# Batch 0's last 192 rows behind four gate products, and gate products over 384 tokens, then 128

## The chip, the cores and the metric

One NeuronCore of one Trainium2 chip runs the whole program. The metric is the time of one execution in microseconds. Three runs of the kernel before give a median of 340.75 us (340.57 to 342.16).

## What is computed

The reference is sliding-window attention with ALiBi slopes, and behind it a gated feed-forward block:

```python
B, H, S, D = 8, 8, 576, 64;  window = 128
scores = q @ k.T / 8 - slope[h] * |i - j|          # only 0 <= i - j < 128
attn   = softmax(scores) @ v                       # per batch and head
x      = attn as 4608 tokens x 512
out    = (gelu(x @ w_gate) * (x @ w_val)) @ w_out  # 512 -> 1536 -> 512
```

Inputs and output are float32 in HBM; the kernel works in bf16 with float32 sums.

## The kernel before

**Tiling.** The 4608 tokens are eight batches of 576. Attention runs batch by batch, the feed-forward block in nine groups of 512 tokens, so group 0 lies wholly in batch 0. The hidden width of 1536 is cut into twelve tiles of 128, called f = 0 to 11. `gate_val(g, f, lo, hi)` makes "one gate product": four matmuls with a tile of `w_gate` and four with the same tile of `w_val`, over tokens lo to hi of group g, then a gelu on ScalarE (L612) and a multiplication into `hT` on VectorE (L613). With its argument `later` the gelu and the multiplication are put in a list and issued where the list is emptied.

**Order.** The order of instructions on each engine is the order in which the code writes them; no scheduler changes it. Every engine takes its own list in order, and waits for semaphores of the others. PSUM has eight banks of 512 columns; `bank()` hands them out in turn as they come free. Loads that turn float32 into bf16 are all issued by GpSimd on one queue. At most eight of them are under way: each issue waits for the one eight places before it.

**The opening stage, batch 0.** Rows 0 to 383 of q and k come first, as float32 on SyncE's and ScalarE's queues, and are cast, transposed on TensorE and scored pair of heads by pair of heads (`c` = 0 to 3; L798 to L808). `exp` (L219) writes the probabilities. Sums over them (`sums_first`), their reciprocals as Ln and Exp on ScalarE (`inverse_first`, L559 and L560), the products with v (`values_first`) and the scaling (`scale_first`, L563) give the tokens 0 to 383 of `xT`.

Batch 0's last 192 rows are a second part. Their q and k are loaded by `load_runs(0, 1, 0, 8)` into the tile `vb[1]`, 64 rows for each of q and k, three tokens to a row. VectorE's cast copy (L814) puts them into `pairs1`, a part of the tile `wo`. `rest` (L761) transposes them and copies them into qT and kT (L158). `scores0_rest` (L348) makes scores and exps for given pairs of heads and puts masks in a list, which `flush` issues (L222). `products_rest` (L573) makes sums and products with v, `inverse_rest` (L582) takes one reciprocal on VectorE for each c (L584), `scale_rest` (L586) makes tokens 384 to 575 of `xT` (L587). So group 0 needs these for its last 128 tokens. Before, the gate products of f = 0 and 1 over 384 tokens stand between the scores of the rest, f = 2 to 8 over 384 tokens behind `products_rest`, then f = 0 to 8 over tokens 384 to 511, then f = 9 to 11 over all 512 (in the loop over g).

`decays` writes the mask's exponentials of a head, `masks_of_last_blocks` copies them to further columns of `emask`. `transpose(1, w, c, copy)` transposes batch 1's q and k on TensorE (L150) once `load_runs(1, n, 0, 8)` has brought them. `preload_act_table_set` loads ScalarE's table for exp and Ln; a gelu behind an exp, or the other way round, has a table load ahead of it.

**Behind it.** The loop over g does the remaining gate products of a group, then the steps of `todo`: scores and values of later batches between the output products (L642, L662).

Of the kernel before, what the change touches and what calls it, by code (L numbers as in the profile page):

```python
# [30 lines left out]
def kernel(  # L31
# [10 lines left out]
    nc = tc.nc  # L42
    B, H, S, D = q.shape
# [72 lines left out]
    def load_v(b, js=range(5)):  # L116
        load(vb[b % 2], v, b, js, 64)
# [12 lines left out]
    def load_runs(b, n, h0, h1):  # L130
        first, parts, r = RUNS[b][n]
        for what, src in ((0, q), (1, k)):
            nc.gpsimd.dma_start(
                out=runs(what, b, n)[:, h0:h1, :],
                in_=src[b][h0:h1, first:first + parts * r, :].rearrange(
                    "h (p r) d -> p h (r d)", r=r))
# [412 lines left out]
    def sums_first(c, u=0):  # L549
        return [(u + x, slice(c, c + 2), n0 * x, n0 * x + n0, 0) for x in (0, 1)]  # L550
# [5 lines left out]
    def inverse_first(c, x, ps):  # L556
        to = recip[0][:, c:c + 2, n0 * x:n0 * x + n0]
        src = ps[:, 0:2 * n0].rearrange("p (c x) -> p c x", c=2)
        return (lambda: nc.scalar.activation(out=to, in_=src, func=AF.Ln),  # L559
                lambda: nc.scalar.activation(out=to, in_=to, func=AF.Exp, scale=-1.0))  # L560
# [143 lines left out]
                   allow_small_or_imprecise_dtypes=True)  # L704
    nc.gpsimd.memset(ones64, 1.0)
    nc.gpsimd.tensor_copy(out=mark, in_=raw[0][0][0:1, 0:2])
    load_runs(0, 1, 0, 8)
    load_v(0, (0, 1, 2))
    load_w(0, 128)
    load_w(128, 256)  # L710
    load_v(0, (3, 4))
    load_w(256, 512)

    for h in range(H):
        nc.vector.memset(slope1[:, h:h + 1], -8.0 * 2.0 ** (-8.0 * (h + 1) / H))
# [45 lines left out]
    def rest(copies):  # L761
        pss = [bank().bitcast(BF16) for _ in range(2)]
        for c in (0, 2):
            for w, ps in enumerate(pss):
                p = 64 * w
                for n in (c, c + 1):
                    for x in range(3):
                        nc.tensor.transpose(
                            out=ps[:, 192 * n + 64 * x:192 * n + 64 * x + 64],
                            in_=pairs1[p:p + 64, x, 128 * n:128 * n + 128],  # L770
                            identity=ident[p:p + 64, p:p + 64])
# [4 lines left out]
    nc.scalar.preload_act_table_set("natural_log_exp_and_others")  # L776
    held = [bank(), bank()]
    keep_busy(held[0], 2, 128)
    keep_busy(held[0], 60)
# [27 lines left out]
    scores0((2,), biases)  # L807
    scores0((3,), biases0((3,)))  # L808
    row(0)
    sums_a = products(0, sums_first(0))  # L810
    for step in zip(*(inverse_first(0, x, sums_a[x]) for x in (0, 1))):
        for do in step:
            do()
    dve(out=pairs1.rearrange("p x (h d) -> p h x d", d=64),  # L814
        in_=vb[1].rearrange("p j x -> p (j x)")[:, 0:1536].rearrange(
            "p (h x d) -> p h x d", h=H, x=3))
    load_w(512, 768)
    load_w(768, 1024)
    load_w(1024, 1280)
    for n in (0, 1):  # L820
        load_runs(1, n, 0, 8)
    load_w(1280, DFF)
    masks, waiting = [], []

    def flush():
# [1 line left out]
            mask(*args)  # L827
        masks.clear()

    rest((dve, dve))  # L830
    sums_b = products(0, sums_first(2))
    for x in (0, 1):
        ln, minus = inverse_first(2, x, sums_b[x])
        ln()
        decays(5 + x, 6 + x)
        minus()
    decays(7, 8)
    vals = products(0, values_first(0) + values_first(2, 2))
# [12 lines left out]
    waiting = waiting[2:] + waiting[:2]  # L851
    for later in waiting:
        later()
    waiting.clear()
    for _ in range(2):
        bank()
    pss = products_rest()
    inverse_rest(0, pss)
    for f in range(2, 9):
        gate_val(0, f, 0, 384)  # L860
        if f < 5:
            inverse_rest(f - 1, pss)
        if f == 5:
            scale_rest()
    masks_of_last_blocks(0, 8)
    for f in range(9):
        gate_val(0, f, 384, 512)
    for n in range(2):
        nc.gpsimd.dma_start(
            out=wo[:, 6 * n:6 * n + 6, :],  # L870
            in_=moe_w_out[768 * n:768 * n + 768, :].rearrange("(c p) f -> p c f", p=128))
# [24 lines left out]
                ("add", b, 2), 4]  # L896


    def exp_table():
        nc.scalar.preload_act_table_set("natural_log_exp_and_others")  # L900

    RUN = {"s": scores, "s2": scores2, "add": add, "sum4": sums4, "gather": gather, "spread": spread_dma, "pv": values, "pv+": values_and_sums,
           "masks": flush, "table": exp_table, "transposes": transposes_dma, "last": out_last, "o": out_half}

    for g in range(NG):
        if 1 <= g < B - 2:
            transposes_dma(3 if g == 1 else g + 2)
        if g == 1:

            nc.gpsimd.tensor_copy(out=mark, in_=qT[1][0:1, 0, 512:514])  # L910
            load_qk(4)
            load_v(3)
        for f in range(9 if g == 0 else 0, NF):
            gate_val(g, f)
            if g == 0 and f in (9, 11):
                for c in (0, 1) if f == 9 else (2, 3):
                    for w in (0, 1):
                        transpose(1, w, c, (act, dve)[w])
# [59 lines left out]
```

## Time and profile before

| what | us |
|---|---|
| median of three runs | 340.75 |
| the profiled execution | 342.65 |
| its span, first to last instruction | 340.8 |
| TensorE matmul busy | 332.9 (98%) |
| VectorE busy | 190.8 (56%) |
| ScalarE busy | 170.1 (50%) |
| GpSimd busy | 106.3 (31%) |
| mean granted TensorE clock | 0.995 |

All times below are counted from the start of the span of that execution. Engines in the profile: PE is TensorE's matmuls, PEld its weight loads, DVE VectorE, ACT ScalarE, POOL GpSimd, SP SyncE. A matmul's end is modelled, so its busy time is not its share of the peak. In the rows the form is: output tile <- input tiles, partitions x elements; buffer numbers are left out.

### The profile page before, as it was taken

How to read it: one execution, taken by the hardware profiler on the slowest of the kernel's cores; microseconds unless marked ns; L12 is line 12 of the kernel's file. 1: busy time of each engine (PE TensorE's matmuls, PEld its weight loads, DVE VectorE, ACT ScalarE, POOL GpSimd, SP SyncE). 2: the span in 40 equal slices, each digit the busy share in tenths (PEclk: the TensorE clock that was granted, in tenths of full speed). 3: DMA queues.
4: the chain of work that ended last, by engine and by line, in shares of the span. 5: the costliest groups of instructions: out<-in, count | busy, mean ns of one | idle time of the engine just before them, and what ended most of it. 6: DMA issues, size and time to landing. Idle time of an engine off the chain costs nothing.

```text
span 340.8 us, 8164 instructions
## 1 busy us (share of the span) xinstructions
PE 332.9 (98%) x3334; PEld 170.4 (50%) x3334; DVE 190.8 (56%) x358; ACT 170.1 (50%) x319; POOL 106.3 (31%) x142
## 2 busy tenths in 40 slices
PE   8899999999998999999999999999999999999996
PEld 6667655444554455445544454445444544444443
DVE  7669566344689637943695369535974323303320
ACT  6973598537894328433753357344823133223322
POOL 5975763481094095007700680040000000000000
PEclk9899999999999999999999999999999999999999
DMA  8999999999699799949993999599106110020002
GB/s 215 164 186 190 205 165 152 141 182 182 135 147 160 146 185 191 185 102 154 182 187 78 165 180 192 75 162 110 64 2 140 63 62 0 3 93 31 0 33 92
DMA packets 149738, 43.49 MB, mean 128 GB/s; under 512 B 133540, under 2 KB 142660, under 8 KB 149700
## 3 DMA queue, kind: packets, MB, share of 16 engines
q0 software_dynamic: 107424, 18.10, 69.0%
q1 hardware_dynamic: 39104, 18.69, 22.8%
q10 hardware_dynamic: 3172, 6.19, 8.3%
q8 instruction: 26, 0.43, 0.5%
q14 instruction: 12, 0.10, 0.1%
HBM read 43.65 MB, written 9.53 MB: 156 GB/s over the span
## 4 chain that ended last, share of the span: by engine, by line
PE 88%; DMA 6%; ACT 2%; DVE 2%; issue 1%; POOL 0%; ACTq 0%; DVEq 0%
PE ps L606 53%; PE ps L642 23%; PE ps L484 4%; DMA rb<-rd 3%; PE ps L288 2%; DMA vb<-in_k_dram 2%; PE ps L662 2%; PE ps L206 1%; DMA wo<-in_q_dram 1%; ACT P L219 1%; PE ps L676 1%; DVE xT L541 1%; PE ps L422 1%; PE ps L150 1%; DVE hT L613 0%
## 5 line engine op out<-in xcount | busy, mean ns | idle before, releaser
L613 DVE TENSOR_TENSOR hT<-ps,gelu 128x512 bf16<-128x512 f32 (+3 forms) x119 | 74.0, 636 | 94.9 <-PE ps L606 89.6
L612 ACT ACTIVATE gelu<-ps 128x512 bf16<-128x512 f32 (+3 forms) x119 | 65.3, 558 | 105.2 <-PE ps L606 95.4
L606 PE MATMUL ps<-xT,wg 128*128 128x512 bf16 (+3 forms) x476 | 113.9, 360 | 0.3
L606 PE MATMUL ps<-xT,wv 128*128 128x512 bf16 (+3 forms) x476 | 113.8, 360 | 0.0
L642 PE MATMUL ps<-wo,hT 128*128 128x512 bf16 x396 | 90.3, 380 | 0.0
L606 PEld LDWEIGHTS <-wv 128*128 128x128 bf16 x476 | 45.6, 98 | 48.6
L606 PEld LDWEIGHTS <-wg 128*128 128x128 bf16 x476 | 44.8, 98 | 48.3 <-issue 0.3
L642 PEld LDWEIGHTS <-hT 128*128 128x128 bf16 x396 | 37.0, 98 | 43.7
L219 ACT ACTIVATE P<-ps 128x512 bf16<-128x512 f32 (+1 forms) x108 | 51.3, 579 | 1.9 <-PE ps L206 1.6
L222 DVE TENSOR_TENSOR P<-P,emask 128x768 bf16<-128x768 bf16 x60 | 31.3, 555 | 19.3 <-ACT P L219 17.7
L647 ACT COPY osb<-ps 128x512 f32<-128x512 f32 x28 | 16.4, 587 | 50.7 <-PE ps L642 50.6
L108 POOL DMA_DIRECT2D vb<-in_v_dram x40 | 34.0, 886 | 6.9 <-DMA ks<-in_k_dram 1.8
L108 POOL DMA_DIRECT2D qs<-in_q_dram x30 | 25.2, 857 | 5.8 <-DMA wo<-in_moe_w_out_dram 4.0
L108 POOL DMA_DIRECT2D ks<-in_k_dram x30 | 25.4, 894 | 0.5 <-DMA qs<-in_q_dram 0.5
L929 POOL COPY mark<-hT 1x2 bf16<-1x2 bf16 x4 | 0.7, 174 | 79.4 <-DVE hT L613 79.4
L541 DVE TENSOR_TENSOR xT<-ps,rb 128x512 bf16<-128x512 f32 (+3 forms) x34 | 14.6, 500 | 6.3 <-PE ps L484 4.8
L484 PE MATMUL ps<-P,vb 64*64 64x192 bf16 (+2 forms) x752 | 17.5, 225 | 0.2
L484 PEld LDWEIGHTS <-vb 64*64 64x64 bf16 x752 | 14.9, 110 | 3.1 <-issue 2.6
L373 DVE TENSOR_TENSOR T<-P 64x1024 bf16<-64x1024 bf16 x20 | 13.7, 686 | 0.6
L288 PEld LDWEIGHTS <-kT 64*64 64x64 bf16 x440 | 7.7, 107 | 4.6 <-issue 4.5
L425 DVE RECIPROCAL r<-ps 128x128 f32<-128x128 f32 (+1 forms) x10 | 9.8, 1020 | 0.0
L612 ACT ACT_TABLE_LOAD x7 | 9.0, 1283 | 1.3 <-PE ps L606 1.3
(90 smaller groups left out, 182.8 us busy)
## 6 DMA issues: line engine op xcount, KB each, us to landing
out_dram<-osb SPq DMA_DIRECT2D x35, 256.0 KB
rb<-rd ACTq DMA_DIRECT2D x10, 576.0 KB
vb<-in_v_dram POOLq DMA_DIRECT2D x32, 128.0 KB, 6.6
qs<-in_q_dram POOLq DMA_DIRECT2D x24, 128.0 KB, 5.7
ks<-in_k_dram POOLq DMA_DIRECT2D x24, 128.0 KB, 6.3
wo<-in_moe_w_out_dram POOLq DMA_DIRECT2D x2, 768.0 KB, 14.8
wg<-in_moe_w_gate_dram POOLq DMA_DIRECT2D x5, 256.0 KB, 8.4
wv<-in_moe_w_val_dram POOLq DMA_DIRECT2D x5, 256.0 KB, 9.0
```

The source lines that it names most:

```text
L108: nc.gpsimd.dma_start(out=t[at:at + n, j, :].rearrange("p (h d) -> p h d", h=H), in_=src[b][:, 128 * j:128 * j + n, :].rearrange("h p d -> ...
L219: nc.scalar.activation(out=dst, in_=src, func=AF.Exp, scale=0.125)
L222: nc.vector.tensor_tensor(out=dst, in0=dst, in1=m, op=ALU.mult)
L288: mm = nc.tensor.matmul(out=ps[64 * x:64 * x + 64, col:col + w], lhsT=keys(b, c, m)[half, :], rhs=qT[b % 2][half, c, q0:q0 + w], start=Tru ...
L373: nc.vector.tensor_tensor(out=to[half, :, x:x + 7:2], in0=P[half, :, 0:10:3], in1=P[half, :, 1:11:3], op=ALU.add)
L484: mm = nc.tensor.matmul(out=out, lhsT=lhsT, rhs=prob(b)[half, c, i, col:col + q1 - q0], start=all(t[2] != u for t in todo[:n]), stop=True, ...
L541: nc.vector.tensor_tensor(out=xT[:, c, at:at + e - a], in0=src, in1=recip[b][:, c, a:e], op=ALU.mult)
L606: nc.tensor.matmul(out=ps, lhsT=w[:, c, 128 * f:128 * (f + 1)], rhs=xT[:, c, t0 + lo:t0 + hi], start=begins, stop=(c == 3), skip_group_che ...
L612: nc.scalar.activation(out=gl[:, 0:n], in_=pg, func=AF.Gelu)
L613: nc.vector.tensor_tensor(out=hid[g][:, f, lo:hi], in0=pv, in1=gl[:, 0:n], op=ALU.mult)
L642: nc.tensor.matmul(out=acc[g], lhsT=hid[g][:, f, 128 * t:128 * (t + 1)], rhs=wo[:, f, :], start=(f == 0), stop=(f == NF - 1))
L647: (nc.vector.tensor_copy if g < B - 2 and t in by_dve.get(g, (0,)) else nc.scalar.copy)(out=osb, in_=acc[g])
```

## The change

Group 0's order is written anew:

- GpSimd loads v's first three blocks and the weights of f = 0 to 3, each as 128 columns, ahead of batch 0's last 192 rows of q and k; v's last two blocks follow.
- The weights of f = 10 and 11 are loaded ahead of batch 1's q and k.
- Both lots of sums follow each other, then all reciprocals, then the remaining decays, then values and scaling.
- Gate products of f = 0 and 1 (two halves of 192 tokens), 2 and 3 (384 tokens) stand ahead of the cast copy, `rest` and the scores of the last rows. An exp table is loaded behind f = 3's gelu, and gelu's again behind the exps.
- f = 4 stands between the scores of the last rows and `products_rest`; f = 5 to 11 over 384 tokens follow. Reciprocals come behind f = 5 to 8, the scaling behind f = 9, the mask copies behind f = 10.
- Then all twelve f over tokens 384 to 511, with batch 1's transposes behind f = 8 and f = 11; the loop over g does no gate product of group 0 any more.

```diff
-    load_runs(0, 1, 0, 8)
     load_v(0, (0, 1, 2))
-    load_w(0, 128)
-    load_w(128, 256)
+    for f in range(4):
+        load_w(128 * f, 128 * f + 128)
+    load_runs(0, 1, 0, 8)
     load_v(0, (3, 4))
-    load_w(256, 512)
...
     row(0)
-    sums_a = products(0, sums_first(0))
-    for step in zip(*(inverse_first(0, x, sums_a[x]) for x in (0, 1))):
-        for do in step:
-            do()
-    dve(out=pairs1.rearrange("p x (h d) -> p h x d", d=64),
-        in_=vb[1].rearrange("p j x -> p (j x)")[:, 0:1536].rearrange(
-            "p (h x d) -> p h x d", h=H, x=3))
     load_w(512, 768)
     load_w(768, 1024)
     load_w(1024, 1280)
+    load_w(1280, DFF)
     for n in (0, 1):
         load_runs(1, n, 0, 8)
-    load_w(1280, DFF)
...
-    rest((dve, dve))
-    sums_b = products(0, sums_first(2))
+    sums = [products(0, sums_first(c)) for c in (0, 2)]
     for x in (0, 1):
-        ln, minus = inverse_first(2, x, sums_b[x])
-        ln()
-        decays(5 + x, 6 + x)
-        minus()
-    decays(7, 8)
+        for c in (0, 2):
+            for do in inverse_first(c, x, sums[c // 2][x]):
+                do()
+    decays(5, 8)
     vals = products(0, values_first(0) + values_first(2, 2))
     for x in (0, 1):
         for c in (0, 2):
             scale_first(c, x, vals[c + x])
-    scores0_rest((0,), masks)
-    gate_val(0, 0, 0, n0, waiting)
-    scores0_rest((1,), masks)
-    gate_val(0, 0, n0, 2 * n0, waiting)
+    for x in (0, 1):
+        for f in (0, 1):
+            gate_val(0, f, n0 * x, n0 * x + n0)
+    gate_val(0, 2, 0, 384)
+    gate_val(0, 3, 0, 384, waiting)
+    dve(out=pairs1.rearrange("p x (h d) -> p h x d", d=64),
+        in_=vb[1].rearrange("p j x -> p (j x)")[:, 0:1536].rearrange(
+            "p (h x d) -> p h x d", h=H, x=3))
+    waiting.pop()()
+    exp_table()
+    rest((dve, dve))
+    scores0_rest((0, 1), masks)
     flush()
     scores0_rest((2, 3), masks)
     flush()
-    gate_val(0, 1, 0, n0, waiting)
-    gate_val(0, 1, n0, 2 * n0, waiting)
-    waiting = waiting[2:] + waiting[:2]
-    for later in waiting:
-        later()
-    waiting.clear()
-    for _ in range(2):
-        bank()
+    gate_val(0, 4, 0, 384)
     pss = products_rest()
-    inverse_rest(0, pss)
-    for f in range(2, 9):
+    for f in range(5, NF):
         gate_val(0, f, 0, 384)
-        if f < 5:
-            inverse_rest(f - 1, pss)
-        if f == 5:
+        if f < 9:
+            inverse_rest(f - 5, pss)
+        if f == 9:
             scale_rest()
-    masks_of_last_blocks(0, 8)
-    for f in range(9):
+        if f == 10:
+            masks_of_last_blocks(0, 8)
...
+    for f in range(NF):
         gate_val(0, f, 384, 512)
+        if f in (8, 11):
+            for c in (0, 1) if f == 8 else (2, 3):
+                transposes_1(c)
...
-        for f in range(9 if g == 0 else 0, NF):
+        for f in range(NF if g == 0 else 0, NF):
             gate_val(g, f)
```

`transposes_1(c)` calls `transpose(1, w, c, ...)` for w = 0 and 1, with the copy of q's on ScalarE and of k's on VectorE, as the loop over g did before.

More of the change, by code (lines that the diff above doesn't have):

```diff
@@ L706 @@
     nc.gpsimd.tensor_copy(out=mark, in_=raw[0][0][0:1, 0:2])
+    load_v(0, (0, 1, 2))
+    for f in range(4):
+        load_w(128 * f, 128 * f + 128)
     load_runs(0, 1, 0, 8)
-    load_v(0, (0, 1, 2))
-    load_w(0, 128)
-    load_w(128, 256)
     load_v(0, (3, 4))
-    load_w(256, 512)
     for h in range(H):
@@ L774, in rest, with exp_table @@
                 untangle(copies[w], 0, 1, w, c, c + 2, ps[:, 192 * c:768])
-    nc.scalar.preload_act_table_set("natural_log_exp_and_others")
+    def exp_table():
+        nc.scalar.preload_act_table_set("natural_log_exp_and_others")
+    exp_table()
     held = [bank(), bank()]
@@ L841 @@
             scale_first(c, x, vals[c + x])
-    scores0_rest((0,), masks)
-    gate_val(0, 0, 0, n0, waiting)
-    scores0_rest((1,), masks)
-    gate_val(0, 0, n0, 2 * n0, waiting)
+    for x in (0, 1):
[7 more added lines that the diff above has]
+    waiting.pop()()
+    exp_table()
+    rest((dve, dve))
+    scores0_rest((0, 1), masks)
     flush()
@@ L848, with transposes_1 @@
     flush()
-    gate_val(0, 1, 0, n0, waiting)
-    gate_val(0, 1, n0, 2 * n0, waiting)
-    waiting = waiting[2:] + waiting[:2]
-    for later in waiting:
-        later()
-    waiting.clear()
-    for _ in range(2):
-        bank()
+    gate_val(0, 4, 0, 384)
     pss = products_rest()
-    inverse_rest(0, pss)
-    for f in range(2, 9):
+    for f in range(5, NF):
         gate_val(0, f, 0, 384)
-        if f < 5:
-            inverse_rest(f - 1, pss)
-        if f == 5:
+        if f < 9:
+            inverse_rest(f - 5, pss)
+        if f == 9:
             scale_rest()
-    masks_of_last_blocks(0, 8)
-    for f in range(9):
+        if f == 10:
+            masks_of_last_blocks(0, 8)
+    def transposes_1(c):
+        for w in (0, 1):
+            transpose(1, w, c, (act, dve)[w])
+    for f in range(NF):
         gate_val(0, f, 384, 512)
+        if f in (8, 11):
+            for c in (0, 1) if f == 8 else (2, 3):
+                transposes_1(c)
     for n in range(2):
@@ L896, in steps @@
                 ("add", b, 2), 4]
-    def exp_table():
-        nc.scalar.preload_act_table_set("natural_log_exp_and_others")
     RUN = {"s": scores, "s2": scores2, "add": add, "sum4": sums4, "gather": gather, "spread": spread_dma, "pv": values, "pv+": values_and_sums,
@@ L912 @@
             load_v(3)
-        for f in range(9 if g == 0 else 0, NF):
+        for f in range(NF if g == 0 else 0, NF):
             gate_val(g, f)
[L915 to L918, printed above, removed]
             if 2 <= g < B - 1:
```

## The prediction

> **What bounds the kernel now.** I read the page's 40 slices first. Each digit is a tenth of a slice of 8.5 us.
>
> ```profile
> PE   8899999999998999999999999999999999999996
> ...
> PEclk9899999999999999999999999999999999999999
> ```
>
> TensorE is busy to nine tenths nearly everywhere, so a change can win only where it isn't. The granted clock has one dip, in the second slice (8.5 to 17 us). Next the chain of work that ended last (start, length, what), cut to the stage that the change touches:
>
> ```profile
> 5.19 6.70 DMA vb<-in_k_dram
> ...
> 19.02 1.63 ACT P L219 x4
> ...
> 22.73 15.20 PE ps L606 x136
> ```
>
> The reader is to see the DMA of batch 0's last 192 rows of k, landed at 11.9, and the exps of the last rows at 19.02. Between the two the chain runs over the cast L814 and the transposes, behind the exps over a table load, a gelu and its multiplication. Only at 22.73 does a run of gate products begin that nothing interrupts. TensorE's timeline (start, length, what, idle before) shows what that costs:
>
> ```profile
> 12.61 0.60 PE L768 MATMUL ps<-ident,wo 64*128 64x64 bf16 x24 [1.05 <-DVE wo L814]
> ...
> 21.29 0.41 PE L484 MATMUL ps<-P,ones 64*64 64x256 bf16 x6 [0.56 <-DVE P L222]
> ```
>
> 1.05 us idle for the cast and 0.56 us for the last mask. And the windows of one microsecond (length, busy time per engine, granted clock as the first number after POOL's):
>
> ```profile
> 14.00:15.00 1.00, 1.00 (x50) 1.00 (x46) 1.00 (x3) 1.00 (x3) 1.00 (x2) 0.60 1.99 170
> 15.00:16.00 1.00, 1.00 (x40) 0.97 (x30) 0.68 (x3) 1.00 (x4) 1.00 (x3) 0.50 2.15 146
> 16.00:17.00 1.00, 1.00 (x9) 0.88 (x7) 1.00 (x3) 1.00 (x4) 1.00 (x2) 0.50 1.48 158
> 17.00:18.00 1.00, 1.00 (x19) 0.62 (x17) 0.85 (x2) 0.26 (x2) 1.00 (x2) 0.69 1.41 179
> ```
>
> The clock fell to half some 3.4 us after the idle began: lost 0.40 + 0.50 + 0.50 + 0.31 = 1.7 us. So some 3.3 us can be won here (1.05 + 0.56 + 1.7), if no new wait comes.
>
> **The skill against the trace.** "TensorE: Matmul & The Clock Gate", Part 1, says that the clock is judged in free-running windows of some 3.4 us, halved after an idle one. The dip, 14.0 to 17.4 by the windows, agrees in length, but the window ahead of it was not idle: 10.6 to 14.0 held two products, a pause and 0.60 us of transposes. I go by the trace: a window about half empty can halve the clock. "ScalarE: Activation LUTs", What ACT_TABLE_LOAD costs, gives some 2.66 us for a switch, drain included. Here:
>
> ```profile
> 20.66 1.28 ACT L612 ACT_TABLE_LOAD   x1
> 21.96 1.09 ACT L612 ACTIVATE gelu<-ps 128x192 bf16<-128x192 f32 x4
> ...
> 45.67 3.23 ACT L219 ACTIVATE P<-ps 128x384 bf16<-128x384 f32 x8
> ```
>
> The load takes 1.28 us, and the gelu starts 0.02 us after it. I take 1.3 us for each of the two loads that are added (exp and gelu around the last rows' exps). The last row gives eight exps of 384 in 3.23 us.
>
> **Part by part.** Times are of the changed kernel, in the same execution's clock. Up to 10.5 nothing on TensorE, ScalarE or VectorE changes its order.
>
> *Loads.* The 192 rows' q and k (384 KB as landed) go from the head of GpSimd's queue behind v (384 KB) and the weights of four products (1,024 KB). Two DMA issues are added (4 x 0.77 us in place of 2 x 0.77).
>
> ```profile
> 21.57 0.87 POOL L133 DMA_DIRECT2D ks<-in_k_dram  x1 [0.41 <-issue]
> ```
>
> k was issued at 5.19 and landed by 11.9, with 384 KB queued up to it. The row is an issue that must wait for the DMA eight places earlier, wv of products 2 and 3: landed by 21.5, with 1,984 KB queued up to it. That is 167 KB per us, so 1,792 KB, the new place of k, land at 11.9 + 1408/167 = 20.3. Bounds: at 195 KB per us (stretch of 24 to 26 us) 19.1, at 154 (10 to 12 us) 21.0. By the same line v is there by 12, the weights of product 3 by 18.1 (needed at some 19), those of 4 and 5 stay where they were (23.9). The last weights move ahead of batch 1's runs: these come 512 KB later, some 3 us, against 35.6 before, and their transposes now start after 41: hidden.
>
> *What TensorE does meanwhile.* The second sums follow the first as soon as the last exp ends (11.90), so 0.4 us idle in place of 1.05. Then values (about 0.95 us at full clock), which end near 13.7. ScalarE has Ln and Exp four times in dependent turns (0.93 us a pair), three decays (0.26 each) and a table load: gelus start near 17.9. VectorE's four scalings (0.47 each) wait for those exps, the last ends near 16.3. Products 0 to 3 start at 14.2, take 2.7 + 2 x 1.30 us and wait some 0.5 for the scalings: they end near 20.0, or 21.0 if the clock halves again at 14. Dropping the two skipped banks removes no instruction. Four gelus of 192 tokens at 0.25, product 2's at 18.9 (0.5) and its multiplication (0.5) keep VectorE until 19.9. The added wait is thus the cast for k, at C = max(19.9, 20.3) = 20.3. Behind it on VectorE stand product 3's multiplication, the four copies and all masks; on TensorE everything from the transposes on.
>
> *From C on*, with VectorE's rows of before:
>
> ```profile
> 11.99 0.56 DVE L814 COPY wo<-vb 128x1536 bf16<-128x1536 bf16 x1 [1.72 <-DMA vb<-in_k_dram]
> 13.16 0.56 DVE L158 COPY qT<-ps 128x384 bf16<-128x384 bf16 x1 [0.61 <-PE ps L768]
> ...
> 25.07 1.34 DVE L584 RECIPROCAL T<-ps 128x192 f32<-128x192 f32 x1
> ```
>
> Cast 11.99 to first copy 13.16, so C+1.17; the copies follow each other by 0.47 and take 0.55, so the second ends at C+2.2, the last at C+3.13. Scores of the first two pairs need the second: C+2.25. From the start of 12 score matmuls to their exp was 0.47 us (17.48 to 17.95): C+2.72. Eight exps: C+5.95. Only 0.9 us of scores and product 4 (1.30) lie beside them, where before two products were spread between. Last mask 0.02 + 0.56: C+6.53, products_rest at C+6.58, for 1.1 us (21.29 to 22.4), so product 5 starts at C+7.7 and ends at E = C+9.0. Table load and gelu of product 4 (C+7.7) hide under that.
>
> *Reciprocals.* They now follow products 5 to 8. A reciprocal and a multiplication take 25.07 to 26.74, 1.675 us, more than a product's 1.30. VectorE starts the first at E+0.62 (product's end 0.20, multiplication 0.42), three pairs later the last at E+5.65, the scaling L587 at E+7.32, done E+8.26. TensorE has six products, E+7.8, and then needs those tokens: waits to E+8.30, 0.5 us. Before, the scaling ended at 31.02 and was needed at 31.83, when the products over 128 tokens began. Behind it: a multiplication, four mask copies (1.42), another multiplication, which frees a bank at E+10.5; TensorE wants it at E+10.3: 0.24 us more.
>
> *The rest.* Twelve products over 128 tokens at 0.449 = 5.4; two lots of batch 1's transposes at 1.15 = 2.3. The 24 extra matmuls (384 + 128 for 512: 162.5 + 56.1 against 216.5 ns) cost 0.05 us. Batch 1's scores start at C + 9.0 + 8.3 + 5.4 + 0.24 + 2.3 = C+25.25 = 45.55; before at 43.71: **+1.8 us**. Behind that point the order is the same and TensorE is packed, so it stays.
>
> *Clock.* From 20.9 to 24.2 TensorE has 0.6 us of transposes, 0.9 of scores and two pauses: as empty as the window that brought the dip. I take half clock up to 27.6, which falls on product 4 (idle time follows: free) and 0.7 us of products_rest: **+0.35**. Bounds: 0, and 1.7 if the half clock falls on a whole window of gate products.
>
> Sum +2.15 us. The profiled execution was 342.65 (span 340.8, 1.85 around it), the median 340.75; the difference is laid on the median: **342.9**. What a measurement can't tell from no change is 0.5%, 1.7 us: 339.05 to 342.45.
>
> **Rivals.** *A, the forecast*, 0.52, itself 342.2 to 344.0.
> *B, better covered*, 0.18: k lands by 19.1, so C is VectorE's 19.9 (-0.4), the clock holds (-0.35) and the bank is free in time (-0.24): 341.9. For it: 195 KB per us is measured from 20 us on. Against: 154 to 178 before.
> *C, late rows and half clock*, 0.20: k at 21.0 (+0.7) and a window of 3.4 us at half clock on dense products (1.7 in place of 0.35): 345.0. For it: more descriptors of small size, since products 2 and 3 now load 128 columns at a time; one dip is there already. Against: the window's phase must fit.
> *D, the other side*, 0.10: rows and VectorE are ready so early that the transposes follow product 3 at once, and the idle time and half clock of before come back with no wait in their place. It decides at C = 20.3 - 2.15 = 18.15; at C = 16 the time is 338.6. For it: the cover of four products is 5.3 us long, and the 3.3 us lost are there. Against: 1,792 KB by 16 is 343 KB per us behind k's old landing, twice what was seen, and ScalarE's table load ends at 17.9.
> That the change doesn't do what it says has no chance of its own: the order of instructions shows each move.
>
> **How the numbers follow.** Faster: 0.06 (most of D). Same: B 0.18, the low end of A 0.06, the rest of D 0.04: 0.28. Slower: 0.66. The range, 341.0 to 345.2, leaves out D and the upper half of C.
>
> **What would show it.** Right: the cast's row with idle time ended by the DMA of k near 20.3; TensorE idle about 1 us ahead of the scores and 1.6 us ahead of products_rest; a wait for VectorE at the first product over 128 tokens. Wrong: the cast before 19, or transposes with no idle time before them; products_rest waiting under 0.5 us; batch 1's scores before 44.

## The result and the profile after

The changed kernel takes 345.27 us (median of 5 runs, 344.70 to 345.82), the kernel before 341.80 beside it (5 runs, 340.57 to 343.19): 3.5 us more by the medians (ratio 1.0112, 95% interval 1.0085 to 1.0138). The forecast was 342.9 (341.0 to 345.2): the right sign, but less than two thirds of the size.

The profiled execution of the changed kernel lasted 344.83 us with a span of 343.0. From the page, the same rows as of before (each digit a tenth of a slice):

```profile
span 343.0 us, 8227 instructions
...
PE   8978799999999999999999999999999999999996
...
PEclk9999999999999999999999999999999999999999
```

The clock's dip in the second slice is gone in this execution. (Of the five, that of 345.27 us has a mean clock of 0.995 again, as the first profile of before.) TensorE now has a 7, an 8 and a 7 in the third to the fifth slice (17 to 43 us), where before there were nines. What stands there is in TensorE's timeline of the changed kernel (start, length, what, idle before and who ended it):

```profile
14.54 0.33 PE L606 MATMUL ps<-xT,wg 128*128 128x192 bf16 x2 [0.35 <-DVE xT L563]
...
21.03 0.60 PE L767 MATMUL ps<-ident,wo 64*128 64x64 bf16 x24 [0.74 <-DVE wo L840]
22.20 0.27 PE L206 MATMUL ps<-qT,kT 64*64 64x192 bf16 x2 [0.57 <-DVE qT L158]
...
26.88 0.41 PE L484 MATMUL ps<-P,ones 64*64 64x256 bf16 x6 [1.17 <-DVE P L222]
...
37.87 0.40 PE L606 MATMUL ps<-xT,wg 128*128 128x128 bf16 x4 [0.48 <-DVE xT L587]
41.40 0.38 PE L606 MATMUL ps<-xT,wv 128*128 128x128 bf16 x4 [1.35 <-DVE hT L613]
```

With three short ones (0.17, 0.20, 0.19) these waits sum to 5.22 us. The two waits of before, 1.05 for the cast and 0.56 for the last mask, have become 0.74 and 1.17, and four new ones of 0.3 us or more stand beside them. The last is the largest and was forecast at 0.24. A bank is waited for there; the multiplication that frees it stands behind the mask copies on VectorE:

```profile
38.20 0.60 DVE L744 COPY emask<-emask 128x1536 bf16<-128x1536 bf16 x1
38.72 0.82 DVE L745 COPY emask<-emask 128x1024 bf16<-128x1024 bf16 x1
39.47 1.30 DVE L748 COPY emask<-emask 64x512 bf16<-64x512 bf16 x2
40.79 2.30 DVE L613 TENSOR_TENSOR hT<-ps,gelu 128x384 bf16<-128x384 f32 x8
```

and GpSimd's timeline of the same kernel at the same time:

```profile
38.48 0.78 POOL L876 MEMSET T<- 64x512 bf16 x1
39.32 0.69 POOL L877 MEMSET P<- 128x512 bf16 x1
40.06 0.55 POOL L879 MEMSET qs<- 64x512 bf16 x1
40.56 0.66 POOL L879 MEMSET ks<- 64x512 bf16 x1
```

Four copies take 2.6 us from the start of the first to the start of the multiplication behind them, where 1.42 was reckoned, and all but the start of the first run while GpSimd fills four tiles. The 1.42 came from these rows of VectorE's timeline of the kernel before (the next multiplication starts at 33.99), where GpSimd issues nothing from 32.32 to 33.47 and fills its tiles only from 38.14 on:

```profile
32.57 0.55 DVE L745 COPY emask<-emask 128x1536 bf16<-128x1536 bf16 x1
33.04 0.42 DVE L746 COPY emask<-emask 128x1024 bf16<-128x1024 bf16 x1
33.38 0.58 DVE L749 COPY emask<-emask 64x512 bf16<-64x512 bf16 x2
```

Batch 1's scores start at 47.23, where 45.55 was forecast and 43.71 was read in the kernel before. Of these 3.52 us between the two profiled executions 2.2 are left at the end: 1.3 are given back in group 2, where the profiled execution of before was slower at two places: a wait of 0.79 us at 109.03, and scores of 1.21 us at 128.65 that take 0.87 in the changed kernel.

### The profile page after: what moved, and what is told of

Same layout as the page of the kernel before. It is cut to its first block, busy times and chain, and to the rows that moved or that the text cites. A ratio compares the mean times of both kernels' runs of the same rounds, so it can differ in the third digit from the quotient of the medians.

```text
span 343.0 us, 8227 instructions
## 1 busy us (share of the span) xinstructions
PE 332.6 (97%) x3358; PEld 171.1 (50%) x3358; DVE 191.6 (56%) x361; ACT 173.7 (51%) x324; POOL 108.4 (32%) x144
## 4 chain that ended last, share of the span: by engine, by line
PE 86%; DVE 3%; DMA 3%; POOL 3%; ACT 2%; issue 2%; DVEq 0%; ACTq 0%
PE ps L606 50%; PE ps L642 24%; PE ps L484 4%; PE ps L288 2%; DMA vb<-in_k_dram 2%; PE ps L662 2%; ACT P L219 1%; PE ps L206 1%; DMA wo<-in_q_dram 1%; PE ps L422 1%; POOL wg L140 1%; POOL wv L140 1%; POOL vb L108 1%; PE ps L676 1%; DVE T L584 1%
## 5 line engine op out<-in xcount | busy, mean ns | idle before, releaser
L484 PEld LDWEIGHTS <-vb 64*64 64x64 bf16 x752 | 14.2, 107 | 3.2 <-issue 2.6
```

Of the source, the lines that this page charges most:

```text
L484: mm = nc.tensor.matmul(out=out, lhsT=lhsT, rhs=prob(b)[half, c, i, col:col + q1 - q0], start=all(t[2] != u for t in todo[:n]), stop=True, ...
```

## The experiments

Theory at this point: the cover that was given up (the scores and two products that ran on TensorE beside the exps and filled its time) costs waits that add up one to one, and the largest is the collision of the mask copies with GpSimd's memsets. Rivals: the rows land too late; the tail (384 tokens, then 128) costs by itself; the waits are covered by others when they are taken away. The kernel before, run on the same chips, had medians of 341.0 to 341.3.

**The mask copies elsewhere** (masks_last): behind all products over 128 tokens.

```
         gate_val(0, f, 0, 384)
         ...
-        if f == 10:
-            masks_of_last_blocks(0, 8)
     ...
+    masks_of_last_blocks(0, 8)
     for n in range(2):
         nc.gpsimd.dma_start(...)
```

> The changed kernel with the mask copies of VectorE moved behind the last product over 128 tokens. Theory A (the wait of 1.35 us in front of the fifth product over 128 tokens is VectorE's mask copies, slowed by GpSimd's memsets): the wait falls under 0.2 us, batch 1's scores start 1.2 us sooner (near 46.0 in place of 47.23), the time falls by about 1.2 us. Rival B (the late rows of k make up nearly all of the loss): under 0.3 us. If the copies meet GpSimd's DMA issues at their new place they are slow there, but no product waits for them.

Measured: 343.14 us (ratio to before 1.0041, 1.0018 to 1.0065), 2.0 above the kernel before beside it, where the changed kernel was 3.5 above. The wait of 1.35 is gone, the others stay (that for the cast is 0.36 here), and gate products of group 1 start at 61.88 instead of 63.29. In VectorE's timeline of this kernel the copies, with nothing waiting for them, are

```profile
46.90 0.87 DVE L744 COPY emask<-emask 128x1536 bf16<-128x1536 bf16 x1
47.69 0.41 DVE L745 COPY emask<-emask 128x1024 bf16<-128x1024 bf16 x1
```

The first is slow here too, beside a DMA issue of GpSimd (0.87 us from 46.53), as was expected. So about 1.5 us of the loss was this wait. From the first product over 128 tokens to group 1 it is 23.91 us in place of 25.42, and the medians, each against before's beside it, differ by 1.45. The 1.51 are more than the listed 1.35 because idle time is counted from the modelled end of the matmuls ahead of it: they start at 39.67, the next would have followed by 0.22, and came at 41.40.

**The memsets elsewhere** (memsets_late): the copies stay, and GpSimd waits for the multiplication of the fifth product over 128 tokens before it fills the tiles.

```
+    nc.gpsimd.tensor_copy(out=mark, in_=hid[0][0:1, 4, 384:386])
     nc.gpsimd.memset(T[64:128, :, 0:64], 0.0)
```

> The changed kernel with GpSimd's four memsets, and the loads of batch 2 behind them, held back until the product of f = 4 over 128 tokens is written; the mask copies stay. Theory A: the four copies take 0.55, 0.42 and 2 x 0.29 us again (1.5 in all in place of 2.6), the wait of 1.35 us falls to about 0.25, as the prediction had it, the time falls by about 1.1 us. Theory C (the copies are long for another reason, for example DMA issues or TensorE's reads): copies and wait stay, time within 0.3 us.

Measured: 343.74 us (1.0071, 1.0052 to 1.0091), 2.6 above before's. VectorE's timeline:

```profile
38.62 0.55 DVE L744 COPY emask<-emask 128x1536 bf16<-128x1536 bf16 x1
39.08 0.42 DVE L745 COPY emask<-emask 128x1024 bf16<-128x1024 bf16 x1
39.42 0.58 DVE L748 COPY emask<-emask 64x512 bf16<-64x512 bf16 x2
```

and TensorE's wait behind them:

```profile
40.64 0.38 PE L606 MATMUL ps<-xT,wv 128*128 128x128 bf16 x4 [0.17 <-DVE hT L613]
```

The copies have their old length and the wait is 0.17, close to the 0.24 of the prediction. This shows the collision: the same copies at the same place, without the memsets beside them. The loads behind the memsets are held back as well, but they can't be the cause: the changed kernel issues none of them before 41.18, when the copies are done. In this run each memset takes 0.52 us. The Trainium skill, "SBUF — State Buffer", SBUF: two separate sides, says that VectorE in a two-port mode and GpSimd take one pair of ports by an exclusive lock, for a whole instruction. The rows agree: 0.82 is 0.42 plus most of a memset, and the memsets grow from 0.52 to 0.78 and 0.69, as if each had waited for the other in turn; whether these copies run in such a mode, no row here says.

**The rows' loads first** (rows_first): the loads of the last 192 rows at their old place at the head of GpSimd's queue, all else as changed.

```
+    load_runs(0, 1, 0, 8)
     load_v(0, (0, 1, 2))
     for f in range(4):
         load_w(128 * f, 128 * f + 128)
-    load_runs(0, 1, 0, 8)
```

> The changed kernel with the loads of batch 0's last 192 rows at the head of GpSimd's queue again, ahead of v and the weights. Rival B: the rows are there by 12, and the time falls by 2 us or more. Theory A: VectorE is busy with product 2 until 19.9 to 20.1, so the cast comes at most 0.5 us sooner and all else stays: 0.3 to 0.5 us. If the weights of f = 0 land later than 14.5 now, it is less.

Measured: 345.04 us (1.0116, 1.0072 to 1.0159), the changed kernel's time. VectorE's timeline:

```profile
20.35 0.60 DVE L840 COPY wo<-vb 128x1536 bf16<-128x1536 bf16 x1
21.16 0.56 DVE L613 TENSOR_TENSOR hT<-ps,gelu 128x384 bf16<-128x384 f32 x1 [0.21 <-PE ps L606]
```

The cast has no idle time before it and still starts at 20.35, since VectorE's multiplications keep it until then. Here the weights behind the rows came late instead (a wait of 0.30 us for w_val at 16.47), which delays those multiplications. In the changed kernel VectorE was free at 20.12 and waited 0.29 us for the DMA: that is all that the late landing cost in this execution.

**The kernel before, once more** (before_again), unchanged, for the scatter of its waits.

> The kernel before, unchanged, profiled again. If half clock near 14 us and the wait of 0.79 us ahead of the first sums of group 2 (near 109 us) are there in only some executions, this profile shows one of them or none and a span of 338.5 to 340.8; if they belong to the kernel, both are there and the span is 340.8 again. The forecast laid a difference worked out in a profile with both on a median of runs; executions without them would account for the median of the change being larger than the difference of the two profiles (2.2 us).

Measured: 341.25 us (1.0005, 0.9980 to 1.0030). But its profiled execution, 340.44 us, differs from the one on which the prediction was built, 342.65. TensorE's timeline of this execution:

```profile
11.46 0.60 PE L768 MATMUL ps<-ident,wo 64*128 64x64 bf16 x24
...
19.62 0.41 PE L484 MATMUL ps<-P,ones 64*64 64x256 bf16 x6 [0.72 <-DVE P L222]
...
33.05 0.38 PE L606 MATMUL ps<-xT,wv 128*128 128x128 bf16 x4 [0.26 <-DVE hT L613]
```

VectorE's:

```profile
10.33 0.83 DVE L814 COPY wo<-vb 128x1536 bf16<-128x1536 bf16 x1
```

The cast starts at 10.33 instead of 11.99 and waits for no DMA, the transposes follow without idle time, the clock stays at 1.0, and the last rows' products start at 19.62 instead of 21.29. This execution is 1.30 us ahead at group 1 and another 0.87 behind group 2, 2.17 in all. So the wait of 1.05 and the half clock, most of the 3.3 us that the change was to win, belong to some executions and not to others. In four profiles with this opening (two of before, tail_alone, tail_weights_again) TensorE's wait for the cast is 1.05, 0, 0.48 and 0, and only the first has half clock near 14 us. How often half clock comes can be read from the mean clock of every run (half clock for 3.4 us of 341 makes 0.995). Of 154 runs of the kernel before, 21 have 0.995 or less, as the first profile has, with a median of 342.67 us; the other 133 have a median of 341.04. So it came, at this place or another, in about one of seven, and these runs took 1.6 us more. All 154 reach from 339.7 to 344.8 us, with a median of 341.2; the first profile's 342.65 lies above 85% of them, the second's 340.44 is faster than nine tenths.

**The tail alone** (tail_alone): the kernel before with the products over 384 tokens up to f = 11, the mask copies after f = 10, all twelve over 128, batch 1's transposes between them. The loads keep their order.

```
-    for f in range(2, 9):
+    for f in range(2, NF):
         gate_val(0, f, 0, 384)
         ...
-    masks_of_last_blocks(0, 8)
-    for f in range(9):
+        if f == 10:
+            masks_of_last_blocks(0, 8)
+    for f in range(NF):
         gate_val(0, f, 384, 512)
+        if f in (8, 11):
+            for c in (0, 1) if f == 8 else (2, 3):
+                transposes_1(c)
```

> The kernel before with the second half of the change alone: gate products f = 2 to 11 over 384 tokens, mask copies behind f = 10, then twelve products over 128 tokens with batch 1's transposes behind f = 8 and 11. Theory A (the tail costs only because the reciprocals now come late and the mask copies meet GpSimd's memsets): here the scaling ends near 31 us and is needed at 35, the copies end near 36, ahead of the memsets at 38: no wait, time as before, within 0.4 us. Rival E (products over 128 tokens cost more than their columns say, or the transposes are late): 0.5 us or more above before.

Measured: 346.95 us (1.0162, 1.0139 to 1.0185), far off the expectation. TensorE's timeline shows one large wait:

```profile
36.83 1.46 PE L606 MATMUL ps<-xT,wg 128*128 128x384 bf16 x4 [4.42 <-DMA wg<-in_moe_w_gate_dram]
```

Products 10 and 11 are wanted some 7 us earlier than before (product 10 from 32.25 in place of 39.01), and their weights lie behind batch 1's rows in GpSimd's queue. Half clock follows, from 36.2 to 39.6 us by the windows; TensorE works in it from 36.83 on and so loses another 1.4 us. All five runs have a mean clock of 0.994 or less. This says nothing of the tail's own price, but it says what the change moves the last weights ahead of batch 1's rows for. Therefore the same with those weights moved (tail_weights_ahead, and again as tail_weights_again):

```
-    for n in (0, 1):
-        load_runs(1, n, 0, 8)
     load_w(1280, DFF)
+    for n in (0, 1):
+        load_runs(1, n, 0, 8)
```

> The kernel before, its opening kept, with the tail of the change (products 2 to 11 over 384 tokens, the mask copies after product 10, all twelve over 128, batch 1's transposes behind the ninth and the twelfth) and, unlike the run before it, the weights of products 10 and 11 loaded ahead of batch 1's rows, as the change has them. Theory A (the tail costs nothing by itself; what the changed kernel loses, it loses between the cast and the scaled values): TensorE does the same columns (a product over 384 tokens recurs every 1.30 us and one over 128 every 0.445, together 1.745, against 1.73 for one over 512), the wait of 4.42 us for the weights is gone, the masks have nobody waiting, and the median stays within 0.6 us of before's (340.8 to 341.9 where before has 341.3). Theory B (the tail has a price of its own: batch 1's rows arrive later and their transposes wait, or the mask copies collide with GpSimd): a wait of 0.5 us or more at batch 1's transposes or at the products over 128, and 342.3 or more.

> The same kernel as the run called tail_weights_ahead, whose one profiled execution lasted 1203 us with every matmul some four times as long as elsewhere, and so cannot be read; its other twelve had a median of 343.3 us, 1.5 above what theory A gave. Theory A (the tail costs nothing): its waits of TensorE sum to no more than those of the kernel before (1.3 us from the first products on), and the median is within 0.6 us of before's. Theory B (the tail has a price of its own of 1 to 2 us): a new wait shows after 30 us, at the products over 128 tokens behind the mask copies, or at batch 1's transposes, or early, where the weights of products 10 and 11 now lie ahead of batch 1's rows; the median is again 342.3 or more.

Measured: 343.26 (1.0045, 1.0018 to 1.0072) and 342.46 us (1.0037, 1.0016 to 1.0058): 1.9 and 1.4 above the kernel before beside them. The first is 343.19 without its profiled execution of 1203 us; why that took so long stayed open. In the second, the tail itself is no slower than before's: from the products of the last rows (20.28) to group 1 (58.65) it takes 38.37 us, against 38.47 and 38.84 in the two profiles of before. So far theory A was right. The median is missed all the same, and in this profile the time is found elsewhere. VectorE's timeline, 70 us later:

```profile
126.32 2.88 DVE L541 TENSOR_TENSOR xT<-ps,rb 128x512 bf16<-128x512 f32 x6 [3.14 <-DMA rb<-rd]
```

The scaling of batch 3's values waits 3.14 us for the DMA that spreads its denominators, and the scores behind it wait for the banks: in TensorE's timeline

```profile
128.85 0.65 PE L288 MATMUL ps<-qT,kT 64*64 64x192 bf16 x26 [0.33 <-DVE xT L541]
```

is the last of four such waits. These 44 scores last from 126.63 to 129.43, where the next products begin: 2.80 us, where they took 0.81 in the second profile of before. There, as in the changed kernel, the same scaling waits for no DMA (0.57 and 0.58 us for TensorE). In the first profile of before it did wait for it, 1.49 us. So in this execution 2.0 us are lost not in the tail's stretch, but where that transfer falls among the others. Without them it would have taken some 340.3 us, less than any of the 22 runs (340.69 or more); most of them must have lost about as much somewhere. Whether there, and whether the tail's order brings it about, one profile can't say: the rival that the tail has a price stands, for all but its own stretch.

**An earlier chain from the cast** (rows_early_use): masks_last, with the rows loaded first, cast and transposed right behind the sums, and the copies out of PSUM behind the scalings, so that only the scores are left behind product 3.

```
+    dve(out=pairs1..., in_=vb[1]...)
+    copy_out = rest((dve, dve))
     decays(5, 8)
     ...
             scale_first(c, x, vals[c + x])
+    copy_out()
     ...
-    dve(out=pairs1..., in_=vb[1]...)
     waiting.pop()()
     exp_table()
-    rest((dve, dve))
```

> masks_last with the last rows loaded first, cast and transposed right behind the sums, and copied out of PSUM behind the four scalings; their scores stay behind product 3. Theory A (from the cast on, a chain of steps runs with nothing beside it: cast, transposes, copies, scores, exps, last mask): the exps can start when ScalarE's exp table is there, near 21.5 in place of 23.1, products_rest starts near 25.4 in place of 27.0, and the time falls by about 1.5 us against masks_last (to 341.6). Rival F (the exps on ScalarE are what counts, the steps ahead of them are hidden by gates): within 0.4 us of masks_last.

Measured: 343.01 us (1.0058, 1.0039 to 1.0077), 1.8 above before's, where masks_last is 2.0 above: no gain that can be told from noise. ScalarE's timeline:

```profile
21.20 1.28 ACT L778 ACT_TABLE_LOAD   x1
22.50 3.17 ACT L219 ACTIVATE P<-ps 128x384 bf16<-128x384 f32 x8
```

and the same two in masks_last:

```profile
20.67 1.28 ACT L776 ACT_TABLE_LOAD   x1
23.16 3.17 ACT L219 ACTIVATE P<-ps 128x384 bf16<-128x384 f32 x8 [1.21 <-PE ps L206]
```

In masks_last the table is there at 21.95, and the exps wait 1.21 us for their scores. Now they start 0.02 us behind the table load with nothing else to wait for, but only 0.66 us sooner, since the table itself comes 0.53 us later. The transposes lie ahead of the first gate product now, which starts at 15.87 in place of 15.02, and the table load has to wait for the gelu of product 3. So a second chain (gates, their gelus, table load) was 1.2 us shorter than the one through the cast, and the work taken out of the one lengthened the other. In the profiles 0.67 us of gain are still there at group 1 (61.21 to 61.88).

**The rest of the chain** (reciprocals_earlier): masks_last, with the reciprocals each a product earlier.

```
     pss = products_rest()
+    inverse_rest(0, pss)
     for f in range(5, NF):
         gate_val(0, f, 0, 384)
-        if f < 9:
-            inverse_rest(f - 5, pss)
-        if f == 9:
+        if f < 8:
+            inverse_rest(f - 4, pss)
+        if f == 8:
             scale_rest()
```

> The changed kernel with the mask copies moved behind all products (343.1 as measured) and the first of the four reciprocals put right behind the products of the last rows, the other three each one product earlier, and the scaling two products earlier. Theory A (the chain from the cast to the scaled values sets the end; its last part is VectorE's alternation of reciprocals and gate multiplications, which began 2.6 us after the products of the last rows were done): the first reciprocal starts at about 28.7 instead of 30.28, the scaling ends at about 36.2 instead of 37.87, the wait of 0.48 us of the first product over 128 tokens is gone, and nothing else moves: TensorE is not ready for those products before 37.4. Median about 342.6, 0.5 below the kernel with the copies moved. Theory B (the earlier reciprocals hold back the multiplications, and so the banks of the products over 384): new waits of TensorE for hT before 37 us, no gain, 343.1 or more.

Measured: 343.00 us (1.0050, 1.0032 to 1.0068). In VectorE's timeline the first reciprocal and the scaling stand where they were expected, if the opening's 0.36 us earlier start in this execution is taken off:

```profile
28.29 1.35 DVE L584 RECIPROCAL T<-ps 128x192 f32<-128x192 f32 x1
...
34.98 0.95 DVE L587 TENSOR_TENSOR xT<-rb,T 128x768 bf16<-128x768 f32 x1
```

and the wait of 0.48 is gone. The medians, each against before's beside it, show 0.4 of the expected 0.5 us (1.7 above, where masks_last is 2.0), less than the width of their intervals (1.2 and 1.6 us): unclear in the time, clear in the trace.

**Product 5 too ahead** (product_ahead_too): as the last run, with `gate_val(0, 5, 0, 384)` moved in front of `products_rest()` and the reciprocals beside products 6 to 8.

> As the run with earlier reciprocals, and product 5 too ahead of the products of the last rows. Theory A: the wait of 1.17 us for the masked exponentials is filled by product 5 (1.30 us), the products of the last rows begin at about 27.1 to 27.4, the first reciprocal at about 29.2, the scaling ends at about 36.8, where TensorE is ready at 36.3, so the first product over 128 tokens begins at 36.8 instead of 37.87: 1.0 us below the kernel with the copies moved, about 342.1 to 342.2 us, still above before's 341.3, since 1.3 us of waits for the transposes' copies and the scores are left. Theory B (the waits are not additive: product 5's bank or its gelu delays the masked exponentials or the copies of the last rows' products): the products of the last rows later than 27.6, and no gain over the run with earlier reciprocals.

Measured: 342.81 us (1.0040, 1.0021 to 1.0058). The wait of 1.17 is filled: the last rows' products start at 27.05, with no wait listed. TensorE's timeline at the products over 128 tokens:

```profile
36.98 0.40 PE L606 MATMUL ps<-xT,wg 128*128 128x128 bf16 x4 [0.61 <-DVE xT L587]
```

They start 0.99 us ahead of masks_last's 37.97, as forecast, and wait again for the scaling: the product was taken out of the stretch that covers the reciprocals. The median is 1.5 above before's, where reciprocals_earlier is 1.7 and masks_last 2.0 above; it misses the 342.1 to 342.2.

**Two trials on the kernel before.** sums_ahead puts the second sums ahead of the last rows' transposes, as the change does; scalar_relieved makes the decays earlier, the scores of two pairs together and the mask copies late.

```
-    rest((dve, dve))
     sums_b = products(0, sums_first(2))
+    rest((dve, dve))
```

```
-    decays(0, 2)
+    decays(0, 5)
     ...
-    decays(2, 4)
+    decays(5, 7)
     ...
-    decays(4, 5)
+    decays(7, 8)
     ...
-        decays(5 + x, 6 + x)
         minus()
-    decays(7, 8)
     ...
-    scores0_rest((0,), masks)
+    scores0_rest((0, 1), masks)
     gate_val(0, 0, 0, n0, waiting)
-    scores0_rest((1,), masks)
     gate_val(0, 0, n0, 2 * n0, waiting)
     ...
-    masks_of_last_blocks(0, 8)
     for f in range(9):
         gate_val(0, f, 384, 512)
+    masks_of_last_blocks(0, 8)
```

> The kernel before with one line moved: the second sums ahead of the transposes of the last rows. Where these rows land late (11.9 in the first profile), the sums fill the wait: 0.7 us less, and 1.7 us more if the clock then holds. Where they land early (10.3 in the second profile), TensorE waits for the last exp instead (0.5 us). Theory A (the scatter of the kernel before, 340.3 to 343, comes from these landings): the median stays within 0.4 us and the runs above 342 become fewer. Rival: the scatter comes from elsewhere and stays.

> A version for speed, from the kernel before: three more of the mask's exponentials in ScalarE's first wait for the loads and none between the reciprocals, scores of the first two pairs of the last rows together, ahead of both products of f = 0; mask copies behind the products over 128 tokens. Theory A (ScalarE is busy without a pause from 9 to 22 us and sets when product 2 can start): its exps start some 0.7 us sooner, product 2 starts near 20.3 in place of 21.07, and 0.26 us of wait at the mask copies go: 0.7 to 1.0 us less than before. If TensorE or VectorE is the bound there: within 0.3 us.

Measured: 341.60 us (1.0014, 0.9996 to 1.0032) and 341.71 us (1.0014, 0.9994 to 1.0034). Neither is faster. In sums_ahead 7 of 22 runs lie above 342 us, of the kernel before beside it 7 of 35: the runs above 342 did not become fewer, so where the scatter of the kernel before comes from stays open. Its profile has other waits in place of the one for the cast (0.58 for the scaling, 0.36 and 0.23 for the first casts); scalar_relieved pays with waits for ScalarE (0.50 at the scores) and for the casts (0.73 and 0.53). No kernel here beats the one before.

**The waits added up.** The waits of TensorE that the timeline lists between 2 and 66 us, one profiled execution each, against the medians. Gaps of 0.16 and 0.22 us that stand where the record of a matmul is missing (listed with "issue") are left out. The difference of waits is to before_again, that of medians to the kernel before that ran beside each.

| kernel | waits, us | more waits than before_again | median more than before |
|---|---|---|---|
| before_again | 1.31 | | |
| changed | 5.22 | 3.9 | 3.5 |
| rows_first | 5.52 | 4.2 | 3.9 |
| memsets_late | 4.10 | 2.8 | 2.6 |
| masks_last | 4.16 | 2.9 | 2.0 |
| rows_early_use | 3.88 | 2.6 | 1.8 |
| reciprocals_earlier | 3.30 | 2.0 | 1.7 |
| product_ahead_too | 2.86 | 1.6 | 1.5 |
| scalar_relieved | 2.32 | 1.0 | 0.5 |
| sums_ahead | 2.09 | 0.8 | 0.4 |

The two columns go together, and no line is off by more than 0.9 us. In the profile the listed waits are nearly all of the loss: 3.9 us, and 0.16 more for each of five additional waits (as seen at the largest one), make 4.7 of the 4.83 us by which group 1 starts later than in before_again. Which waits would be there in another execution, this can't say; and tail_weights_again (1.62 here, and its loss at 126 us) has its time elsewhere.

## Why the prediction was wrong

*Steps that held.* The cast started at 20.41 (20.3 said), with VectorE free at 20.12 (19.9) and k landed 0.29 us after that. The scores that need the second copy at C+2.26 (2.25), exps at C+2.65 (2.72), the last rows' products at C+6.47 (6.58), product 5 at C+7.7 (7.7), the wait of 0.48 for the scaling (0.5), the first product over 128 tokens at 37.87 (37.6). Products 0 to 3 waited 0.35 for the scalings (0.5). Both table loads were hidden. The tail's own stretch cost nothing in the profile (0.05 said), though the tail alone is 1.4 to 1.9 us slower in the medians. The signs named for "right" came: idle time of the cast ended by the DMA, 0.96 us ahead of the scores (1 said), 1.17 ahead of the last rows' products (1.6 said), and VectorE waited for at the first product over 128 tokens. None of them stood at the step that failed.

*First failed step: "four mask copies (1.42) [...] 0.24 us more".* The copies took 2.59 us, and the wait was 1.35 us as listed, 1.51 from product to product. The copies' lengths were taken from a place where GpSimd filled no tiles, and the change moves them by 5.6 us on top of GpSimd's memsets, which stay where they were (38.14 before, 38.48 now). The prediction names no work of GpSimd there. memsets_late gives the 0.17 that the step would have been right about. This is 1.3 of the 1.7 us that batch 1's scores came later than forecast; the first product over 128 tokens (0.27) and pieces too small to name are the rest.

*Second failed step: "the difference is laid on the median".* The difference was made against one execution of 342.65 us, 1.9 above that median of three and 1.4 above that of 154 runs, and the excess was not neutral: it lay in the very waits that the change was to remove, the 1.05 for the cast and the 1.7 of half clock; six of seven runs don't have the latter. In before_again neither is there. Against that execution the last rows' products of the changed kernel start 7.26 us later (26.88 to 19.62), where the first profile has 21.29 and a difference of 5.59. Of these 1.7 us 1.3 are left at group 1: booked as a gain, and none in an execution like that one. For the same reason "so it stays", said of all that follows batch 1's scores, failed: 1.3 us were given back at waits that the first profile happened to have.

*A term that did not come: the clock, +0.35.* The prediction took a stretch "as empty as the window that brought the dip" to bring another. From 20.5 to 23.9 us TensorE of the changed kernel is busy for 1.91 us of 3.40, less than the 2.23 of 3.40 ahead of the dip of before (10.8 to 14.2), and no window from 14 to 27 us is below 1.00. So how empty the stretch is did not decide it alone. The dip itself was also misread: in windows of 0.2 us it runs from 14.2 to 17.6, and it began 2.6 us after the idle time did (11.56), not 3.4; the 3.4 us are its length. Without this term the forecast would have been lower still.

*The sum.* Against the second profile of before, at group 1: +1.84 said, 1.7 for late scores and 1.3 for the first profile's late start of group 1 make 4.8, which is 63.29 less 58.46. From there to the 3.5 of the medians, 0.45 are given back in group 2, and the profiled executions lie 1.4 (before_again, 340.44) and 0.4 us (changed, 344.83) below the medians of the first comparison: 4.83 - 0.45 - 1.36 + 0.44 = 3.46. Against the first profile the sum looks right, 342.65 + 2.15 = 344.80 with 344.83 measured, but that is luck: 1.7 us of late scores stand against 0.35 of clock and 1.3 given back. In the medians the first step alone is as large as the miss: masks_last, which mends it, is 2.0 above before, and the forecast without its 0.24 is 1.9. How the two steps divide the loss of a median execution is not shown.

*The rivals.* C named 345.0, but by rows at 21.0 and half clock, and neither came in the profiled execution: the number was near for reasons that were wrong. Of B the clock held, but not the bank, and rows_first shows that the earlier landing brings nothing, as VectorE is not free before. D needed rows and VectorE before 18.15; VectorE never was.

## What to carry to other kernels

A profile of one execution shows waits that come and go: before a change is priced by the wait that it removes, see whether an execution at the median has that wait, or at least lay the difference on the profiled execution's own time as the other bound (here 344.8). The mean clock of many runs tells how often half clock comes, without a profile. When instructions move in time, look at what every other engine does at the new time, those whose own list has not changed included. And work that is taken out of one chain lengthens the one that it is put into (rows_early_use), and products used as cover ahead of a chain are missing behind it (product_ahead_too).

## What the runs showed of the hardware

VectorE's bf16 copies within SBUF and GpSimd's memsets lengthen each other: copies from 0.42 to 0.82 and from 0.58 to 1.30 for two, memsets 0.52 to between 0.55 and 0.78. VectorE's multiplications with an operand in PSUM, beside the same memsets in masks_last and tail_weights_again, left the memsets at 0.52. Beside GpSimd's DMA issues copies were longer too: the first mask copy took 0.96 us in tail_alone where 0.55 is its length, with an issue of 0.88 us begun at 39.89, a little before it. In before_again the last two took 0.96 in place of 0.58 beside an issue of 1.12 us begun at 31.16, and the wait of 0.26 at 33.05 follows.

Half clock was seen twice, for 3.4 us each: from 14.2 to 17.6 in the first profile of before, and from 36.2 to 39.6 in tail_alone. In the 3.4 us ahead of it TensorE was busy for 2.23 us in the first case and not at all in the second; 1.91 us of 3.40 in the changed kernel (20.5 to 23.9) brought none.

The scaling at 126 us, whose instructions are the same in all these kernels, waited for the spreading DMA not at all in the second profile of before and in the changed kernel, 1.49 us in the first profile of before and 3.14 us in tail_weights_again.
